# Score blocks for VectorE as four-column products of masked q, w2 on another queue, and a new plan of numbers

## The chip, the cores and the metric
The kernel runs on one core of a Trainium2 chip. The core has TensorE (PE; its weight loads are listed as PEld), VectorE (DVE), ScalarE (ACT), GpSimd (POOL) and SyncE (SP), which only issues DMAs here; ScalarE can issue DMAs on a queue of its own. All five run their own instruction streams and wait for each other by semaphores. The metric is the device time of one execution in microseconds (us); lower is better. The median before is 662.22 us.

## The reference, cut to what matters
```python
x = A_x                                  # 1 x 2048 x 512, bf16
xn = layernorm(x)
q = (xn @ wq), 32 heads of 16            # scale 16 ** -0.5 on the scores
k, v = xn @ wk, xn @ wv                  # one head of 16, shared by all 32
p = softmax(q @ k.T)                     # 32 heads x 2048 x 2048 scores
s = (p @ v, heads side by side) @ wo
g = silu(silu(xn @ w1) @ w2)             # 512 -> 1792 -> 512
out = x + s * g
```
The softmax has 134 million exponentials. They are the bulk of the work outside TensorE.

## The kernel before, in words
The queries are cut into 4 column blocks of 512 (c), and the heads into groups of four, which gives 8 groups a block and 32 groups (gi) in all. In a group, head i of four lies on partitions 32i to 32i+31 of `qT_sb`, 16 of them its own; a pair of groups shares the 32 partitions, and `kT_sb` exists twice (`kTa`, `kTb`), with k on the lower or the upper 16 of each 32 and zeros elsewhere, so that the even group of a pair is met by kTa and the odd one by kTb. `kTb` is made by small DMAs from `kTa` (`move_K`, L501).

For each group, keys come in 16 tiles of 128 (kt). A *block* is the scores of one head, one key tile and 512 queries, keys on the partitions: one matmul with 32 contracted rows at row position 32i (`score`, `burst`, L613). Two blocks fill one of the two halves psA0, psA1 of PSUM and are exponentiated by one ScalarE instruction of 1024 columns into one of NPA slots of `pa_sb` (`exp_A`, L643; "an exp" below). Other key tiles go to VectorE: four blocks of one tile, each in one of the banks D, D1 (psD) or F (psF), are turned by one add with an int16 output into bits of a bf16 power of two (`exp_D`, L681); GpSimd makes two shifted copies of the four (`shift`, L706, INT64_ADD), and the three weighted copies together stand for the exponential. The probabilities never leave the core: each block is multiplied with v (and a column of weights for the sum) into psO, 32 columns for each of the four heads side by side (`emit_PV`, L765). Four such matmuls, one per head, make a *quad*; they use the four column positions of TensorE at once, while score matmuls use the four row positions. The PE stream is therefore a sequence of *score runs* (row form: one psA half and one or two blocks for VectorE that ride along) and *stretches* between them (column form: value quads and pieces of the dense work).

The dense work (q of the next block, h = xn @ w1, z = u @ w2, the output product w) is cut into four-column products as well (`columns`, L392) and fills the stretches, through bank F. Its silu takes a tanh on ScalarE (L1081) and products on VectorE (L1113, L1125, then the addition of x, L1092, and a store from `ob_sb`).

Nothing of this order is written out by hand. The class `Sched` records every operation with what it reads and writes, gives it a planned time from fixed costs, and derives the semaphores. The main loop (L1353 on) decides at each step, by those planned times, how many quads and dense pieces go into the next stretch, which blocks ride in the next run, and what VectorE does next. A string `PLAN` names a row of `RULES` for every 5 us of planned time; a row holds the thresholds for these decisions (waiting times, how many stretches to keep ahead, how much dense work may lag, and so on). Changing a number therefore changes the order of thousands of instructions.

DMAs are recorded the same way and go to SP's queue in the recorded order: the kTb moves, w1, the late loads (`late_loads`: wo, w2; both on SP), reloads of x, and the stores. `fill_D` (L1308) picks the VectorE blocks that ride in a run; `extra_fill` (L1288) can put one between runs, in row form; `col`-form filling of VectorE blocks doesn't exist.

## Time and profile before
| | |
|---|---|
| Median of 3 runs | 662.22 us (661.94 to 662.23) |
| The profiled execution | 662.46 us, of which its span (first to last instruction) 660.6 us |
| ScalarE busy | 652.5 us, 99%; 662 exps at 1217 ns mean, 72 tanhs at 797 ns mean |
| TensorE busy | 648.8 us, 98% |
| VectorE busy | 597.3 us, 90% |
| GpSimd busy | 382.9 us, 58% |
| Granted TensorE clock | 1.00 |
| First exp starts, last exp ends | 10.21 us, 653.23 us |

The page gives for each engine the time in which at least one of its instructions ran. ScalarE and TensorE overlap the end of one instruction with the start of the next, so their mean durations are longer than the distance from one to the next, and a share near 100% still can hide short waits. The chain of waits goes back from the last instruction to what released each step; a line of it gives the start, the length and what ran, so its steps show distances and not durations. "Idle before" is the time an engine stood still ahead of an instruction, with what ended it.

### The profile page before, as it was taken

Reading aid. Unit: us, or ns where it says so; the run is one execution under the profiler, and the core shown is the slowest. Engines: PE = TensorE matmul, PEld = TensorE weight load, DVE = VectorE, ACT = ScalarE, POOL = GpSimd, SP = SyncE. Lnnn points to the kernel's source line nnn. Section 1 sums busy time; section 2 is a strip of 40 time slices with the busy share of each in tenths; the row PEclk is TensorE's granted clock in tenths of the full one; section 3 lists DMA queues with packets and bytes.
Section 4 is the critical chain, followed back from the end, with each engine's and each line's share of the span. In section 5 each row is a group of like instructions: output and inputs, shape, how many; then the busy total and the mean of one; then the engine's idle time right before and its main releaser. Section 6 shows DMA issues by size and latency. Waiting matters only on the chain.

```text
span 660.6 us, 18424 instructions
## 1 busy us (share of the span) xinstructions
PE 648.8 (98%) x8061; PEld 182.9 (28%) x8061; DVE 597.3 (90%) x1021; ACT 652.5 (99%) x754; POOL 382.9 (58%) x387
## 2 busy tenths in 40 slices
PE   8999999999999999999999999999999999999996
PEld 4422222222222222222222222222222222222222
DVE  7998899998899989999998989999989888898996
ACT  8999999999999999999999999999999999999997
POOL 3265666655566567566656655575656555665554
PEclk9999999999999999999999999999999999999999
DMA  5440000000000000000000000010000000000110
GB/s 167 153 147 1 2 1 2 2 1 2 2 1 2 17 18 18 17 2 2 1 2 1 2 1 2 2 33 18 18 1 3 1 2 2 1 2 2 33 34 33
DMA packets 12320, 12.48 MB, mean 19 GB/s; under 512 B 2512, under 2 KB 11728, under 8 KB 12240
## 3 DMA queue, kind: packets, MB, share of 16 engines
q1 hardware_dynamic: 11680, 10.78, 5.3%
q8 instruction: 63, 1.03, 0.7%
q10 hardware_dynamic: 560, 0.52, 0.2%
q14 instruction: 17, 0.14, 0.1%
HBM read 8.95 MB, written 2.10 MB: 17 GB/s over the span
## 4 chain that ended last, share of the span: by engine, by line
ACT 91%; PE 4%; DVE 2%; issue 1%; DMA 1%; SPq 1%; POOL 0%; POOLq 0%
ACT pa_sb L643 85%; ACT t_sb L1081 5%; PE psA L613 1%; DMA x_sb<-in_A_x_dram 1%; PE psO L765 1%; DVE ph_sb L681 1%; DVE stats_sb L408 0%; POOL ph_sb L706 0%; PE psD L452 0%; PE psF L392 0%; DMA kTb_sb<-kTa_sb 0%; SPq L501 0%; PE psD L483 0%; DVE kTa_sb L495 0%; POOLq L293 0%
## 5 line engine op out<-in xcount | busy, mean ns | idle before, releaser
L643 ACT ACTIVATE pa_sb<-psA 128x1024 bf16<-128x1024 f32 x662 | 630.5, 1217 | 0.9 <-PE psA L613 0.6
L706 POOL INT64_ADD ph_sb<-ph_sb x290 | 300.3, 1048 | 192.7 <-DVE ph_sb L681 192.6
L681 DVE TENSOR_SCALAR ph_sb<-psD 128x512 int16<-128x512 f32 (+1 forms) x520 | 349.1, 689 | 33.7 <-PE psD L613 29.8
L765 PE MATMUL psO<-ph_sb,vaug_sb 128*32 128x512 bf16 x1740 | 215.9, 383 | 0.1
L765 PE MATMUL psO<-pa_sb,vaug_sb 128*32 128x512 bf16 (+1 forms) x1332 | 200.2, 383 | 0.4 <-ACT pa_sb L643 0.4
L613 PE MATMUL psA<-qT_sb,kTa_sb 32*128 32x512 bf16 x688 | 133.4, 385 | 1.9 <-DVE kTa_sb L495 0.5
L613 PE MATMUL psD<-qT_sb,kTb_sb 32*128 32x512 bf16 x353 | 129.5, 384 | 0.0
L613 PE MATMUL psA<-qT_sb,kTb_sb 32*128 32x512 bf16 x628 | 121.7, 385 | 2.2 <-ACT pa_sb L643 1.7
L613 PE MATMUL psD<-qT_sb,kTa_sb 32*128 32x512 bf16 x309 | 111.6, 384 | 0.2
L706 POOL INT64_ADD x_sb<-x_sb x72 | 74.5, 1046 | 52.2 <-DVE x_sb L681 52.1
L681 DVE TENSOR_SCALAR x_sb<-psD 128x512 int16<-128x512 f32 (+1 forms) x132 | 90.1, 690 | 10.6 <-PE psD L613 8.9
L765 PE MATMUL psO<-x_sb,vaug_sb 128*32 128x512 bf16 x432 | 73.7, 383 | 0.0
L613 PEld LDWEIGHTS psA<-qT_sb,kTa_sb 32*128 32x128 bf16 x688 | 32.3, 91 | 141.8 <-ACT pa_sb L643 125.5
L392 PE MATMUL psF<-xnT_sb,w_sb 128*32 128x512 bf16 x896 | 71.1, 385 | 0.0
L392 PE MATMUL psF<-w_sb,u_sb 128*32 128x512 bf16 x896 | 69.2, 384 | 0.0
L613 PEld LDWEIGHTS psA<-qT_sb,kTb_sb 32*128 32x128 bf16 x628 | 29.5, 91 | 134.4 <-ACT pa_sb L643 124.4
L765 PEld LDWEIGHTS psO<-ph_sb,vaug_sb 128*32 128x32 bf16 x1740 | 52.5, 95 | 49.7 <-issue 34.1
L765 PEld LDWEIGHTS psO<-pa_sb,vaug_sb 128*32 128x32 bf16 x1332 | 48.1, 94 | 41.9 <-issue 32.1
L1081 ACT ACTIVATE t_sb<-psF 128x512 bf16<-128x512 f32 x72 | 57.4, 797 | 0.0
L1113 DVE SCALAR_TENSOR_TENSOR u_sb<-t_sb,psF 128x512 bf16<-128x512 bf16 x56 | 38.0, 679 | 4.7 <-ACT t_sb L1081 4.2
L681 DVE TENSOR_SCALAR ph_sb<-psF 128x512 int16<-128x512 f32 x52 | 35.4, 681 | 0.0
L613 PEld LDWEIGHTS psD<-qT_sb,kTb_sb 32*128 32x128 bf16 x353 | 30.9, 91 | 3.5 <-DVE ph_sb L681 2.5
(128 smaller groups left out, 341.6 us busy)
## 6 DMA issues: line engine op xcount, KB each, us to landing
w_sb<-in_B_w_dram SPq DMA_DIRECT2D x2, 1792.0 KB, 8.8
x_sb<-in_A_x_dram SPq DMA_DIRECT2D x18, 128.0 KB, 2.3
out_dram<-ob_sb SPq DMA_DIRECT2D x14, 128.0 KB, 1.7
x_sb<-in_A_x_dram SPq DMA_DIRECT2D x3, 512.0 KB, 7.1
wop_sb<-in_A_wo_dram SPq DMA_DIRECT2D x1, 512.0 KB, 4.0
wq_sb<-in_A_wq_dram SPq DMA_DIRECT2D x1, 384.0 KB, 6.6
x_sb<-in_A_x_dram ACTq DMA_DIRECT2D x2, 128.0 KB, 2.9
kTb_sb<-kTa_sb SPq DMA_DIRECT2D x16, 16.0 KB, 2.3
```

The lines of the kernel that those rows point to most:

```text
L392: r = e.matmul(bank[32 * i:32 * i + 32, :], lhsT=lhsT[:, 32 * i:32 * i + 32], rhs=rhs, start=start, stop=stop, tile_position=(0, 32 * i), ...
L613: return e.matmul(ap, lhsT=kT_sb[g % 2][32 * i:32 * i + 32, kt * P:(kt + 1) * P], rhs=qT_sb[32 * i:32 * i + 32, c % 2, g // 2, :], start=T ...
L643: d = op("a", lambda e: e.activation(pa_sb[:, sl, :], psA[k][:, :], ACT.Exp, scale=ESCALE), reads=["A%d" % k], writes=[("pa", sl)], cost=2 ...
L681: d = op("v", lambda e: e.tensor_scalar(ph_ap(0, sl, 512 * pos, 512 * pos + m), src, float(PH_ONE + PH_BIAS), 0.0, op0=ALU.add, op1=ALU.ma ...
L706: d = op("gp", lambda e, j=j: e.int64_add(ph_ap(j, sl, 0, 4 * NQ).bitcast(I64), ph_ap(0, sl, 0, 4 * NQ).bitcast(I64), PH_SHIFT[j] * 0x0001 ...
L765: r = e.matmul(psO[32 * i:32 * i + 32, cs], lhsT=vaug_sb[:, p["v"], p["kt"], :], rhs=p["ap"], start=s0, stop=s1, tile_position=(0, 32 * i) ...
L1081: op("a", lambda e: e.activation(t_sb[:, n % 2, :], bank_ap(b), ACT.Tanh, scale=0.5 if jb[0] == "h" else 0.25), reads=[b], writes=[("t", n ...
L1113: op("v", lambda e: e.scalar_tensor_tensor(out=dst, in0=t_sb[:, n % 2, :], scalar=1.0, in1=src, op0=ALU.add, op1=ALU.mult), reads=tk["read ...
```

## The change
Seven things are changed together:
- A tensor `qm_sb` [128, 4, 512] is added, zeroed once on GpSimd in the start. For each pair of groups four DMAs on SP (`mask_q`) copy head i's 32 rows of q into `qm_sb[32i:32i+32, i, :]`. The other rows stay zero, so a product over all 128 rows of kT with `qm_sb[:, i, :]` is head i's score block. It can be made in column form: four matmuls of 32 columns (`col_fill`, through `columns`).
- The main loop may put such a *column fill* into a stretch (`col_want` looks whether a bank is free and whether VectorE would have a block earlier by more than a threshold, CGAIN or CLEFT).
- The load of w2 is issued on ScalarE's queue instead of SP's.
- NPA goes from 11 to 10 slots.
- The gated result is written to `ob_sb` directly, and x is added to it there; `fin_sb` is gone.
- `held` counts by a dictionary (no instruction of the chip changes by that).
- PLAN and RULES are new, with two more numbers a row.

```diff
-    NPA = 11
+    NPA = 10
...
-        fin_sb = sb("fin_sb", [P, 2, D])
+        qm_sb = sb("qm_sb", [P, 4, NQ])
...
+        op("gp", lambda e: e.memset(qm_sb[:], 0.0), writes=[("qm", i) for i in range(4)], cost=1.8)
...
-            op("sp", lambda e: e.dma_start(w2_sb[:], B_w2.rearrange("(ft p) n -> p ft n", p=P)), writes=["w2"], lane="lw2", cost=9.0)
+            op("a", lambda e: e.dma_start(w2_sb[:], B_w2.rearrange("(ft p) n -> p ft n", p=P)), writes=["w2"], lane="lw2", cost=9.0)
...
-                op("v", lambda e: e.scalar_tensor_tensor(out=fin_sb[:, tt % 2, :], in0=src, scalar=0.25,
+                op("v", lambda e: e.scalar_tensor_tensor(out=ob_sb[:, tt % NOB, :], in0=src, scalar=0.25,
...
+        def mask_q(gi):
+            c, h = gi // NG, (gi % NG) // 2
+            for i in range(4):
+                op("sp", lambda e, i=i: e.dma_start(qm_sb[32 * i:32 * i + 32, i, :], qT_sb[32 * i:32 * i + 32, c % 2, h, :]),
+                   reads=[("qT", c % 2, h), "qTb"], writes=[("qm", i)], lane=f"qm{i}")
+            qm["of"] = gi // 2
...
+        def col_fill(w):
+            _, bank, o, i = w
...
+            def f(e):
+                return columns(e, bank_ap(bank), kT_sb[gi % 2][:, kt * P:(kt + 1) * P], qm_sb[:, i, :], True, True)
+            ks = [("kT", 1, kt // 2, n) for n in range(4)] if gi % 2 else [("kT", 0, kt // 2 if kt else "first")]
+            op("pe", f, reads=[("qm", i)] + ks, writes=[bank], cost=("col", [0, 1, 2, 3], NQ))
+            dst["fifo"].append(dict(tile=o["tile"], i=i, bank=bank, idx=idx, pos=pos, rows=o["rows"]))
+            hold[bank] = "blk"
+            return 1
...
+                w = col_want(t, CGAIN) if CGAIN < 9 and slots > did else None
+                k = int((w[0] - max(t, K.pe_next("col")) - 0.05) / 0.2163 + 0.8) if w else 9
+                if k <= 0:
+                    did += col_fill(w)
...
+                if CLEFT < 9 and slots > did:
+                    w = col_want(max(t, K.pe_next("col")), CLEFT)
+                    if w and w[0] <= max(t, K.pe_next("col")) + 0.1:
+                        did += col_fill(w)
```

More of the change, by code (lines that the diff above doesn't have):

```diff
@@ L254, in bass_recurrent_scan__grouped_kv_mqa__dense_activation_silu__prompt_kernel @@
     NPAIR, LEAD_PAIR = 1, 1
+    COLS, CGAIN, CLEFT = 1, 9, 9
     TWIN = 0
@@ L262, in bass_recurrent_scan__grouped_kv_mqa__dense_activation_silu__prompt_kernel @@
     PLAN = (
-        "AAAAJAVDBHQUALNMAMMPRULHALUHROAAMAKVIAVMMASMAAAAAFVIAAKAANJM"
-        "AGGHQLHSNAMAAGMPOCVAVAMAAVIAAHLAMRHIAFHKTOLENGTNLUAAAAPAPHRA"
-        "ESJA"
+        "AAAAHbEbOAZQHCFBAAYARBZMAVTAAAbMBZIYAUBWOQADVAJGPFTAUAHFXAGW"
+        "AABNWZAAFAYQaZQJXQbALZScFAACNZFANQZMGZZYAGAAAZVZQAAAAFZAAZKA"
+        "QA"
     )
     RULES = dict(
-        A=(0.2, 3.0, 0.65, 10, 1.2, 2.0, 0, 12, 0.2, 3, 3, 0.0, 9, 0.43, 0, 0.33, 0, 0),
-        B=(0.1, 3.0, 0.65, 10, 1.2, 2.0, 0, 12, 0.2, 3, 3, 0.0, 9, 0.43, 0, 0.33, 0, 0),
@@ L270, in bass_recurrent_scan__grouped_kv_mqa__dense_activation_silu__prompt_kernel @@
-        C=(0.3, 3.0, 0.65, 10, 1.2, 2.0, 0, 12, 0.2, 3, 3, 0.0, 9, 0.43, 0, 0.33, 0, 0),
-        D=(0.2, 3.0, 0.5, 10, 1.2, 2.0, 0, 12, 0.2, 3, 3, 0.0, 9, 0.43, 0, 0.33, 0, 0),
-        E=(0.2, 3.0, 0.65, 9, 1.2, 2.0, 0, 12, 0.2, 3, 3, 0.0, 9, 0.43, 0, 0.33, 0, 0),
-        F=(0.2, 3.0, 0.65, 11, 1.2, 2.0, 0, 12, 0.2, 3, 3, 0.0, 9, 0.43, 0, 0.33, 0, 0),
-        G=(0.2, 3.0, 0.65, 10, 1.2, 2.0, 4, 12, 0.2, 3, 3, 0.0, 9, 0.43, 0, 0.33, 0, 0),
-        H=(0.2, 3.0, 0.65, 10, 1.2, 2.0, 8, 12, 0.2, 3, 3, 0.0, 9, 0.43, 0, 0.33, 0, 0),
@@ L276, in bass_recurrent_scan__grouped_kv_mqa__dense_activation_silu__prompt_kernel @@
-        I=(0.2, 3.0, 0.65, 10, 1.2, 2.0, 0, 12, 0.2, 3, 3, 0.04, 9, 0.43, 0, 0.33, 0, 0),
-        J=(0.2, 3.0, 0.65, 10, 1.2, 2.0, 0, 12, 0.2, 3, 3, 0.0, 0.05, 0.43, 0, 0.33, 0, 0),
-        K=(0.2, 3.0, 0.65, 10, 1.2, 2.0, 0, 12, 0.2, 3, 3, 0.0, 0.15, 0.43, 0, 0.33, 0, 0),
-        L=(0.2, 3.0, 0.65, 10, 1.2, 2.0, 0, 12, 0.2, 3, 3, 0.0, 0.25, 0.43, 0, 0.33, 0, 0),
-        M=(0.2, 3.0, 0.65, 10, 1.2, 2.0, 0, 12, 0.2, 3, 3, 0.0, 0.35, 0.43, 0, 0.33, 0, 0),
-        N=(0.2, 3.0, 0.65, 10, 1.2, 2.0, 0, 12, 0.2, 3, 3, 0.0, 9, 0.43, 0.2, 0.33, 0, 0),
@@ L282, in bass_recurrent_scan__grouped_kv_mqa__dense_activation_silu__prompt_kernel @@
-        O=(0.2, 3.25, 0.65, 10, 0.6, 2.0, 0, 12, 0.2, 3, 3, 0.0, 0.05, 0.43, 0, 0.33, 0, 0),
-        P=(0.1, 2.5, 0.65, 10, 1.2, 2.0, 4, 12, 0.2, 3, 3, 0.0, 9, 0.43, 0, 0.33, 2, 0),
-        Q=(0.2, 2.5, 0.65, 10, 1.2, 2.0, 0, 12, 0.2, 3, 3, 0.0, 0.15, 0.43, 0, 0.33, 0, 0),
-        R=(0.2, 3.0, 0.65, 10, 1.2, 2.0, -12, 12, 0.2, 3, 3, 0.04, 9, 0.43, 0, 0.33, 0, 0),
-        S=(0.2, 3.0, 0.65, 10, 1.2, 3.0, 0, 6, 0.2, 2, 3, 0.0, 9, 0.43, 0, 0.33, 0, 0),
-        T=(0.2, 3.0, 0.65, 10, 1.2, 2.0, 0, 12, 0.2, 3, 2, 0.0, 9, 0.43, 0, 0.6, 2, 0),
@@ L288, in bass_recurrent_scan__grouped_kv_mqa__dense_activation_silu__prompt_kernel @@
-        U=(0.2, 3.0, 0.65, 10, 1.2, 2.0, 0, 12, 0.2, 3, 3, 0.0, 9, 0.55, 0, 0.33, 1, 0),
-        V=(0.2, 3.0, 0.65, 10, 1.2, 2.0, 0, 12, 0.2, 2, 4, 0.04, 9, 0.43, 0, 0.33, 0, 1),
+        A=(0.2, 3.0, 0.65, 10, 1.2, 2.0, 0, 12, 0.2, 3, 3, 0.0, 9, 0.43, 0, 0.33, 0, 0, 9, 9),
+        B=(0.2, 3.0, 0.65, 10, 1.2, 2.0, 0, 12, 0.2, 3, 3, 0.0, 9, 0.43, 0, 0.33, 0, 0, 0.4, 9),
+        C=(0.2, 3.0, 0.65, 10, 1.2, 2.0, 0, 12, 0.2, 3, 3, 0.0, 9, 0.43, 0, 0.33, 0, 0, 0.6, 9),
+        D=(0.2, 3.0, 0.65, 10, 1.2, 2.0, 0, 12, 0.2, 3, 3, 0.0, 9, 0.43, 0, 0.33, 0, 0, 0.8, 9),
@@ new lines, in bass_recurrent_scan__grouped_kv_mqa__dense_activation_silu__prompt_kernel @@
+        E=(0.2, 3.0, 0.65, 10, 1.2, 2.0, -12, 12, 0.2, 3, 3, 0.0, 9, 0.43, 0, 0.33, 0, 0, 9, 9),
+        F=(0.2, 3.0, 0.65, 10, 1.2, 2.0, 0, 12, 0.2, 3, 3, 0.0, 9, 0.43, 0.2, 0.33, 0, 0, 9, 9),
+        G=(0.2, 3.0, 0.65, 10, 1.2, 2.0, 0, 12, 0.2, 3, 3, 0.0, 9, 0.43, 0, 0.33, 1, 0, 9, 9),
+        H=(0.2, 3.0, 0.65, 10, 1.2, 2.0, 0, 12, 0.2, 3, 3, 0.0, 0.05, 0.43, 0, 0.33, 0, 0, 9, 9),
+        I=(0.2, 3.0, 0.65, 10, 1.2, 2.0, 0, 12, 0.2, 3, 3, 0.0, 9, 0.43, 0, 0.33, 2, 0, 9, 9),
+        J=(0.2, 3.0, 0.65, 7, 1.2, 2.0, 0, 12, 0.2, 3, 3, 0.0, 9, 0.43, 0, 0.33, 0, 0, 9, 9),
@@ new lines, in bass_recurrent_scan__grouped_kv_mqa__dense_activation_silu__prompt_kernel @@
+        K=(0.2, 3.0, 0.65, 10, 1.2, 2.0, 0, 24, 0.2, 3, 3, 0.0, 9, 0.43, 0, 0.33, 0, 0, 9, 9),
+        L=(0.2, 3.0, 0.65, 10, 1.2, 2.0, -8, 12, 0.2, 3, 3, 0.0, 9, 0.43, 0, 0.33, 0, 0, 9, 9),
+        M=(0.2, 3.0, 0.65, 10, 1.2, 2.0, 0, 12, 0.2, 3, 3, 0.0, 0.25, 0.43, 0, 0.33, 0, 0, 9, 9),
+        N=(0.25, 3.0, 0.6, 10, 1.2, 2.0, 0, 12, 0.2, 3, 4, 0.0, 9, 0.43, 0, 0.33, 0, 0, 0.6, 9),
+        O=(0.2, 3.0, 0.65, 10, 1.2, 2.0, 0, 12, 0.2, 3, 3, 0.0, 9, 0.43, 0, 0.15, 0, 0, 0.8, 0.05),
+        P=(0.25, 3.0, 0.65, 10, 1.2, 2.0, 0, 12, 0.2, 3, 3, 0.0, 0.35, 0.43, 0, 0.33, 0, 1, 9, 9),
@@ new lines, in bass_recurrent_scan__grouped_kv_mqa__dense_activation_silu__prompt_kernel @@
+        Q=(0.2, 2.75, 0.65, 10, 1.2, 2.0, 0, 12, 0.2, 3, 3, 0.0, 9, 0.43, 0.2, 0.33, 0, 0, 0.6, 9),
+        R=(0.2, 3.0, 0.65, 10, 1.2, 2.0, 0, 12, 0.2, 3, 3, 0.04, 9, 0.43, 0, 0.33, 2, 0, 9, 0.05),
+        S=(0.2, 3.0, 0.65, 10, 0.6, 2.0, 0, 12, 0.3, 3, 4, 0.0, 9, 0.43, 0, 0.33, 0, 0, 0.8, 9),
+        T=(0.2, 3.0, 0.65, 10, 1.2, 2.0, 0, 12, 0.2, 2, 3, 0.0, 9, 0.43, 0, 0.15, 0, 0, 9, 0.05),
+        U=(0.2, 3.0, 0.65, 10, 1.2, 2.0, 0, 12, 0.2, 3, 3, 0.04, 9, 0.43, 0, 0.33, 0, 0, 9, 0.4),
+        V=(0.2, 3.0, 0.65, 10, 1.2, 2.0, 0, 12, 0.2, 3, 4, 0.0, 9, 0.43, 0, 0.6, 0, 0, 0.4, 0.6),
@@ new lines, in bass_recurrent_scan__grouped_kv_mqa__dense_activation_silu__prompt_kernel @@
+        W=(0.2, 3.25, 0.65, 10, 1.2, 2.0, 0, 12, 0.2, 4, 3, 0.0, 9, 0.43, 0, 0.33, 0, 0, 0.6, 0.4),
+        X=(0.25, 3.0, 0.65, 10, 1.2, 3.0, 0, 12, 0.2, 3, 3, 0.0, 9, 0.43, 0, 0.6, 0, 0, 0.6, 0.4),
+        Y=(0.2, 2.75, 0.65, 10, 1.2, 1.5, 0, 12, 0.2, 3, 3, 0.0, 9, 0.43, 0, 0.33, 0, 0, 0.4, 9),
+        Z=(0.2, 3.0, 0.65, 10, 1.2, 3.0, 4, 12, 0.2, 3, 3, 0.0, 9, 0.43, 0, 0.15, 0, 0, 9, 0.05),
+        a=(0.3, 3.0, 0.65, 10, 1.2, 2.0, -4, 24, 0.2, 3, 3, 0.04, 9, 0.43, 0, 0.33, 0, 0, 9, 9),
+        b=(0.2, 3.25, 0.65, 10, 1.2, 2.0, 0, 12, 0.2, 4, 3, 0.04, 9, 0.43, 0, 0.33, 0, 1, 9, 9),
@@ L290, in bass_recurrent_scan__grouped_kv_mqa__dense_activation_silu__prompt_kernel @@
+        c=(0.2, 3.0, 0.7, 10, 1.6, 2.0, 0, 12, 0.2, 3, 3, 0.0, 9, 0.43, 0, 0.33, 0, 0, 0.6, 9),
     )
@@ L593, in bass_recurrent_scan__grouped_kv_mqa__dense_activation_silu__prompt_kernel @@
             halves[gi] = [(h, (2 * p, 2 * p + 1), rows) for h in range(2) for p in range(NPAIR) for rows in ([0, 1], [2, 3])]
-        pend = [[] for _ in range(NGRP)]
+        pend, waiting = [[] for _ in range(NGRP)], {}
         npv = [[0] * 4 for _ in range(NGRP)]
@@ L628, in held @@
         def held(key):
-            return any(p["key"] == key for q in pend for p in q)
+            return waiting.get(key, 0) > 0
         def owe(gi, i, kt, v, ap, key, at, half=None):
             pend[gi].append(dict(i=i, kt=kt, v=v, ap=ap, key=key, at=at, half=half))
+            waiting[key] = waiting.get(key, 0) + 1
         def fill_A(tile, rows, k):
@@ L754, in emit_PV @@
                     pend[gi] = [x for x in pend[gi] if x is not p]
+                    waiting[p["key"]] -= 1
                     owed[gi] -= 1
@@ L1054, in emit_job @@
                 else:
-                    task(k, evac, 0.69, jb=jb, bank=b, reads=[b], writes=[])
+                    task(k, evac, 0.69, jb=jb, bank=b, reads=[b], writes=[("ob", jb[1] % NOB)] if k == "w" else [])
                 if k in ("z", "w"):
@@ L1099, in add @@
             tt = tk["jb"][1]
-            final_add("v", tt, fin_sb[:, tt % 2, :], ("fin", tt % 2))
+            final_add("v", tt, ob_sb[:, tt % NOB, :], ("ob", tt % NOB))
             tok.add(("add", tt))
@@ L1124, in evac @@
                 tt = jb[1]
-                op("v", lambda e: e.scalar_tensor_tensor(out=fin_sb[:, tt % 2, :], in0=src, scalar=0.25,
+                op("v", lambda e: e.scalar_tensor_tensor(out=ob_sb[:, tt % NOB, :], in0=src, scalar=0.25,
                                                          in1=tmp_sb[:, (tt // 4) % 2, tt % 4, :],
                                                          op0=ALU.mult, op1=ALU.mult),
-                   reads=[b, ("tmp", tt % 8)], writes=[("fin", tt % 2)], cost=tk["cost"])
+                   reads=[b, ("tmp", tt % 8)], writes=[("ob", tt % NOB)], cost=tk["cost"])
                 tok.add(("wev", tt))
-                task("add", add, 0.42, jb=jb, reads=[("fin", tt % 2), ("x", 12 + tt % 4)], writes=[])
+                task("add", add, 0.42, jb=jb, reads=[("ob", tt % NOB), ("x", 12 + tt % 4)], writes=[])
             elif k == "wp":
@@ L1138, in bass_recurrent_scan__grouped_kv_mqa__dense_activation_silu__prompt_kernel @@
         dst = dict(open=[], idx=-1, fifo=[])
+        qm = dict(of=-1)
         ast = dict(tile=None, rows=None)
@@ L1306, in extra_fill, with col_want @@
             fill_D(best[0], [0, 1, 2, 3], [best[1]])
+        def mask_q(gi):
[4 more added lines that the diff above has]
+            qm["of"] = gi // 2
+        def col_want(t, least):
+            if front or group_A() >= NGRP or sum(held(("pa", k)) for k in range(NPA)) >= XHOLD:
+                return None
+            pick = next(((o, i) for o in dst["open"] for i in o["todo"]
+                         if o["tile"][0] // 2 == qm["of"] and K.ready("pe", [("qm", i)]) <= t), None)
+            if pick is None:
+                return None
+            vfree = K.free["v"] + 0.62 * len(dst["fifo"])
+            ride = max(needed(), t + 0.2) + 0.43
+            best = None
+            for b in BANKS:
+                if hold[b] is None and (b != "F" or not jobs or not behind(F_BEHIND) or not next_job(t)):
+                    r = max(t, K.ready("pe", [], [b]))
+                    gain = max(vfree, ride) - max(vfree, r + 0.43)
+                    if gain > least and (best is None or r < best[0]):
+                        best = (r, b) + pick
+            return best
+        def col_fill(w):
+            _, bank, o, i = w
+            (gi, kt), idx = o["tile"], o["idx"]
+            pos = len(o["rows"]) - len(o["todo"])
+            o["todo"].remove(i)
+            if not o["todo"]:
+                dst["open"].remove(o)
+            def f(e):
[5 more added lines that the diff above has]
+            return 1
         def fill_D(t, free, only=None):
@@ L1332, in fill_D @@
                         dst["open"].append(dict(tile=new, todo=list(rows), rows=rows, idx=dst["idx"]))
+                        if COLS and not front and new[0] // 2 > qm["of"] and all(x["tile"][0] // 2 == new[0] // 2 for x in dst["open"]):
+                            mask_q(new[0])
                         pick = [(dst["open"][-1], i) for i in free if i in rows] or [(dst["open"][-1], rows[0])]
@@ L1354, in bass_recurrent_scan__grouped_kv_mqa__dense_activation_silu__prompt_kernel @@
             (SLIP, ROUND, KEEP, HOLD, AGES["gn1"], AGE, F_BEHIND, ENDQ, PVWAIT, LEAD, AHEAD, MARGIN, XGAIN, AIM, TWIN,
-             TGATE, FRESH, JOINT) = \
+             TGATE, FRESH, JOINT, CGAIN, CLEFT) = \
                 RULES[PLAN[min(int(K.act_end / STRETCH), len(PLAN) - 1)]]
@@ L1404, in bass_recurrent_scan__grouped_kv_mqa__dense_activation_silu__prompt_kernel @@
                     did += 2
+                w = col_want(t, CGAIN) if CGAIN < 9 and slots > did else None
+                k = int((w[0] - max(t, K.pe_next("col")) - 0.05) / 0.2163 + 0.8) if w else 9
+                if k <= 0:
+                    did += col_fill(w)
                 if slots > did:
-                    did += emit_PV(max(t, K.pe_last + K.pe_len) + 0.08, slots - did)
-                if can and not dense_first and slots > did:
-                    did += emit_job(t, slots - did)
+                    did += emit_PV(max(t, K.pe_last + K.pe_len) + 0.08, min(k, slots - did) if k > 0 else slots - did)
+                if can and not dense_first and slots > did and k > 0:
+                    did += emit_job(t, min(k, slots - did))
+                if w and k > 0 and slots > did and w[0] <= K.pe_next("col") + 0.12:
+                    did += col_fill(w)
+                    if slots > did:
+                        did += emit_PV(max(t, K.pe_last + K.pe_len) + 0.08, slots - did)
+                if CLEFT < 9 and slots > did:
+                    w = col_want(max(t, K.pe_next("col")), CLEFT)
+                    if w and w[0] <= max(t, K.pe_next("col")) + 0.1:
+                        did += col_fill(w)
             if TWIN and more and not blocked and did and not front and tanh_ready(K.act_end - TWIN):
```

## The prediction
> **What bounds the kernel now.** I read the page's busy line first, then the groups, the busy time by stretches, the chain of waits and the DMA view by window.

> ```profile
> span 660.6 us, 18424 instructions
> PE 648.8 (98%) x8061; PEld 182.9 (28%) x8061; DVE 597.3 (90%) x1021; ACT 652.5 (99%) x754; POOL 382.9 (58%) x387
> ...
> L643 ACT ACTIVATE pa_sb<-psA 128x1024 bf16<-128x1024 f32 x662 | 630.5, 1217 | 0.9 <-PE psA L613 0.6
> ...
> L1081 ACT ACTIVATE t_sb<-psF 128x512 bf16<-128x512 f32 x72 | 57.4, 797 | 0.0
> ```

> ScalarE is 99% busy, nearly all of it 662 exponentials (exps, L643) and 72 tanhs. By stretches (PE, PEld, DVE, ACT, POOL, clock, DMA, GB/s):

> ```profile
> 40.00:140.00 100.00, 99.23 (x1225) 27.55 (x1226) 92.44 (x156) 100.00 (x117) 59.36 (x58) 1.00 0.03 9
> ...
> 540.00:640.00 100.00, 99.79 (x1280) 26.49 (x1276) 91.04 (x149) 100.00 (x113) 60.03 (x58) 1.00 0.04 12
> sum 600.00, PE 596.28 PEld 162.46 DVE 548.66 ACT 600.00 POOL 360.24; mean PE 99.38 PEld 27.08 DVE 91.44 ACT 100.00 POOL 60.04
> ```

> For 600 us ScalarE is never idle. But a mean of 1217 ns hides gaps below 0.3 us: an exp starts before the one ahead has ended. The pitch tells them, so I take it from the chain, and count the start against it in ScalarE's timeline (the line by itself):

> ```profile
> 26.98 0.62 PE psF L452 x8
> 27.60 0.33 PE psO L765 x4
> 27.93 0.32 PE psA L613 x2
> ...
> 32.84 1.80 DMA kTb_sb<-kTa_sb
> ...
> 34.69 0.39 PE psF L613
> 35.08 0.33 PE psO L765 x4
> 35.40 0.32 PE psA L613 x2
> ...
> 35.78 17.51 ACT pa_sb L643 x19
> 53.29 0.49 ACT t_sb L1081
> ...
> 610.15 25.67 ACT pa_sb L643 x28
> ```

> ```profile
> 10.21 35.75 ACT L643 ACTIVATE pa_sb<-psA 128x1024 bf16<-128x1024 f32 x38 [0.59 <-PE psA L613]
> ```

> Pitch of an exp: 25.67 / 28 = 0.917 us; a tanh adds 0.49. The 38 exps from 10.21 would take 1.02 (the first one's own row) + 37 x 0.917 = 34.95; they took 35.75, so 0.8 us of stalls. From 45.96 to the last exp's end at 653.23 lie 624 exps and 72 tanhs: 572.2 + 35.3 = 607.5 against 607.3: no stall at all. The span is therefore head 10.2 + exps and tanhs 642.2 + stalls 0.8 + tail 7.3. Two stalls show their cause in the chain. The exp fed by the run at 27.93 came 0.23 late: transposes (0.62) and a value quad (0.33) stood ahead of its score run. The one fed at 35.40 came 0.14 late: TensorE waited at 34.64 for a kTb move to land.

> **The change, part by part.**
> *ScalarE's and VectorE's work.* The order of the built program has the same 662 exps, 72 tanhs, 724 blocks for VectorE (704 single evacuations and 10 pairs before, 708 and 8 after) and 362 INT64_ADDs. VectorE takes no block more than before; so 642.2 us stay: 0.
> *48 column fills.* 48 of the 724 single score matmuls outside psA become four 32-column products (192 matmuls, L392's helper), in the stretch of the value quads instead of riding in the score run. Price in TensorE time from the chain: a run is 0.32, a stretch of quads 0.33 for one and 0.22 for each further one (x4 0.33, x8 0.55). From exp 47 on, the order has 1387 quads in 615 gaps before (2.26 each) and 1433 after (2.33): 0.32 + 0.33 + 0.22 x 1.26 = 0.93 grows to 0.94 a gap. A gap has 0.917 + 72/615 x 0.49 = 0.974. Over stretches of 50 gaps the fullest had 98% before (gaps 546 to 595, no stall) and 98% after (gaps 296 to 345): ScalarE hides it, 0.
> *The two stalls.* In the new order the value quad ahead of the late run is gone (0.33 less, more than the 0.23), and the first block that needs the last kTb move stands four exps later (3.7 us): -0.23 - 0.14 = -0.37.
> *Tail.* Before, a value quad (0.22) stood between the last score run and the products for VectorE's first half of the last normalisation; after it stands earlier. That half starts 0.22 sooner, but the second half needs the last exp (653.23) and its product (653.29 + 0.40), so it starts at 653.74 instead of 653.87: -0.13. The last INT64_ADD pair stands two exps earlier; POOL is not the end.
> *w2 on ScalarE's queue*, after 23 exps, at about 30.7 us. No row shows ScalarE issuing between two exps. Lower end 0: an issue takes 0.51 (SP's row for w2) and the pitch is 0.917. Upper end: the issue waits for the datapath, 0.51 + the lost overlap 0.30 = 0.8. I take 0, by the exps' own rows: the next one is handed over 0.30 before the last has ended, so the queue runs ahead.
> *64 mask copies on SP* (32 KB each, 0.59 to issue by the kTb moves; four take 2.4 us, and the last lands 1.8 after its issue). In SP's queue only stores and x reloads stand between the batches, and what waits behind a mask is those. A mask can go once the pair before has read its row for the last time; by the order its first use comes 8 exps (7.3 us) or more after that, so the 2.4 + 1.8 are hidden, except in the first four. Those meet loads:

> ```profile
> kTb_sb<-kTa_sb SPq DMA_DIRECT2D x4, 16.0 KB, 5.0
> ...
> kTb_sb<-kTa_sb SPq DMA_DIRECT2D x4, 16.0 KB, 1.8
> ```

> The moves issued behind the w1 load (17.84 us) took 5.0 to land, those with nothing before them (31.02) 1.8. The first masks now stand behind wop, and w2 runs beside wop. Before, w2 (issued at 34.1, landed after 9.6) moved its 1.8 MB in the 6.2 us after wop's landing at 37.5: 300 GB/s. Started at about 32, some 1.1 MB of it are left when wop's 0.5 MB start at 34.5. The four x tiles at the start, two on each queue, landed alike (2.7 and 2.9 us), so I let the queues share: at half the rate wop lands at about 38.9 and the second mask at about 39.3. Its use stands ahead of the 33rd exp's run, which may start at 39.2 (11.23 + 30 x 0.917 + 0.45 of stalls). Estimate: the run is late by 0.45, of which some 0.1 is slack: +0.35. Lower end 0 (the loads don't slow each other: mask at 37.9). Upper end: masks behind all of w2, as the moves behind w1: about 41, +1.8. I take 0.35, by the x tiles. The last four kTb moves run beside w2 too; they are first needed at about 38 now, 3.4 after today's landing, and cost only in that upper case, in the same hole. [...]
> *Memset of qm on POOL*: 1.80 by kTb's, from 5.24 (wkp's copy ends) to 7.04, in the head:

> ```profile
> 3.09 1.80 POOL L377 MEMSET kTb_sb<- 128x2048 bf16 x1
> 4.84 0.40 POOL L379 COPY wkp_sb<-wkn_sb 128x256 bf16<-128x256 bf16 x1
> ...
> 6.13 1.38 DVE L441 TENSOR_SCALAR xn_sb<-x_sb,mv_sb,rstd_sb 128x512 bf16<-128x512 bf16 x4
> ```

> POOL's next work is at 11.41, so on POOL 0. But the four normalisations at 6.13, on the path to the first exp, now lie inside it. Lower end 0: kTb's memset ran beside three BATCH_NORM_STATS2 at the usual 0.69. Upper end: all VectorE work waits for 7.04, 0.91, and with the reciprocal at 5.91 about 1.1. I take 0, the memset's own row being the nearest; the other case is a rival.
> *The rest* goes together: ob instead of fin (same 12 + 12 instructions; the store four tiles back lands in 1.7 us, tiles are microseconds apart), NPA 10 (a slot comes round after 9 us), the counter in held (host only): 0.
> Sum: -0.37 - 0.13 + 0.35 = -0.15 on the profiled execution's 662.46 (span 660.6 and 1.9 around it): 662.3. It stands 0.24 above the median of the three runs, 662.22; so I predict 662.1 for a median.

> **The rivals.**
> *POOL's memset holds VectorE in the head.* For: VectorE's SBUF products (L853) range from 407 to 793 ns, and POOL is busy beside them. Against: the kTb memset's row. It gives 662.1 + 0.9 = 663.0, still within the bound below. [...]
> *The issue of w2 holds ScalarE*: 662.1 + 0.8 = 662.9. Against: the overlap of the exps.
> *Column fills make TensorE late (slower).* The view of waits (us in total, times, longest) has weight loads for psD standing for VectorE to free the bank, 0.25 each:

> ```profile
> PEld psD L613 <- DVE ph_sb L681: 6.7, 27, 0.4
> ```
>  Today they stand behind psA's run and delay no exp; a column fill stands ahead of it. It decides once some six of the 48 are held by that 0.25 with no slack left (1.5 us); with a quarter of them, 12 x 0.25 = 3.0: 665.1. For: gaps are 97% full where the fills are dense. Against: fuller gaps ran without a stall.
> *Faster.* The change doesn't do what it says, in the sense that VectorE's share does not grow. To win 1.3 us it would have to save all stalls (0.8), the tail's 0.13 and 0.4 more, for which I see no place: 660.8.

> **How the numbers follow.** 0.2% is 1.3 us, about what a measurement of this kernel can tell from no change. Likeliest case 0.52 (662.1); memset 0.22 (663.0); w2's issue 0.08 (662.9); slower rival 0.15 (665.1); faster 0.03 (660.8). The first three lie within 0.2%: 0.82. Range: downwards the sum without the 0.35 and 0.3 more of the early stalls (661.4), upwards the memset's and the masks' upper parts together (663.5); outside lie the slower and the faster case, 0.18.

> **What would show it.** ScalarE's chain unbroken at 0.917 from some 45 us on; ten or so first exps alike; no late exp near 29 and 37, one of 0.3 near 40 with TensorE waiting for a qm copy; first exp at 10.2 (11.1 if the memset holds). Wrong would be: exps late by 0.1 to 0.4 all along, behind products that read qm, with VectorE as releaser; or a hole of 0.8 at about 31.

## The result, and the profile after

The changed kernel takes 666.98 us (median of five runs, 664.41 to 668.03), against 661.94 (661.81 to 662.23) before: ratio 1.0069, 95% interval 1.0047 to 1.0092. It is slower, and its runs spread over 3.6 us where those of before spread over 0.4. The prediction said 662.1, no change. Three single runs far off the others (801.64 us with w2 later, 686.62 with both mends, 982.71 with w2 alone on ScalarE's queue), at a mean clock of 0.66 to 0.85, stand in no median or range below.

The page of the kernel after, busy times, granted clock and the two groups that make up ScalarE's work:

```profile
span 665.2 us, 18816 instructions
...
PE 652.6 (98%) x8199; PEld 184.7 (28%) x8201; DVE 597.5 (90%) x1023; ACT 652.6 (98%) x754; POOL 384.2 (58%) x388
...
PEclk9979999999999999999999999999999999999999
...
L653 ACT ACTIVATE pa_sb<-psA 128x1024 bf16<-128x1024 f32 x662 | 630.9, 1220 | 5.0 <-PE psD L622 2.8
...
L1092 ACT ACTIVATE t_sb<-psF 128x512 bf16<-128x512 f32 x72 | 57.8, 803 | 0.0
```

The numbers of instructions are as forecast, 662 and 72. The idle time ahead of the exps went from 0.9 to 5.0 us, and one slice of the clock row reads 7. ScalarE's timeline (start, us, engine, line, operation, xcount, idle before) says where:

```profile
10.80 20.28 ACT L653 ACTIVATE pa_sb<-psA 128x1024 bf16<-128x1024 f32 x22 [0.59 <-PE psA L622]
30.92 8.41 ACT L653 ACTIVATE pa_sb<-psA 128x1024 bf16<-128x1024 f32 x9
40.39 1.02 ACT L653 ACTIVATE pa_sb<-psA 128x1024 bf16<-128x1024 f32 x1 [1.07 <-PE psD L622]
43.00 1.02 ACT L653 ACTIVATE pa_sb<-psA 128x1024 bf16<-128x1024 f32 x1 [1.58 <-PE psA L622]
44.94 1.02 ACT L653 ACTIVATE pa_sb<-psA 128x1024 bf16<-128x1024 f32 x1 [0.92 <-PE psD L622]
46.46 1.02 ACT L653 ACTIVATE pa_sb<-psA 128x1024 bf16<-128x1024 f32 x1 [0.50 <-PE psD L622]
47.82 7.44 ACT L653 ACTIVATE pa_sb<-psA 128x1024 bf16<-128x1024 f32 x8 [0.34 <-PE psD L622]
```

Five exps in a row are late, by 1.17, 1.69, 1.02, 0.60 and 0.44 us against the pitch of 0.917: 4.93 us, "the hole" below. The other 728 exps and tanhs keep the pitch to 0.01 us, from the first at 10.80 to the last, which ends at 657.95. The books: first exp later by 0.59 (10.80 for 10.21); early stalls gone, -0.80; hole +4.93; tail 7.24 for 7.34, -0.10. That makes 4.62, and the spans differ by 665.2 - 660.6 = 4.6.

What TensorE waited for at 36 to 50 us (total, times, longest), and then the stretches with busy time of each engine, granted clock, DMA share and GB/s:

```profile
PE psD L401 <- DMA qm_sb<-qT_sb: 1.1, 1, 1.1
PE psF L622 <- DMA kTb_sb<-kTa_sb: 0.8, 1, 0.8
```

```profile
36.00:38.00 2.00, 2.00 (x24) 0.50 (x21) 1.83 (x3) 2.00 (x3) 0.70 (x2) 1.00 1.10 368
38.00:40.00 2.00, 1.10 (x11) 0.33 (x9) 0.95 (x2) 1.33 (x2) 1.98 (x2) 1.00 1.09 344
40.00:42.00 2.00, 0.88 (x15) 0.27 (x11) 1.74 (x3) 1.02 (x1) 0.00 (x0) 0.67 0.30 72
42.00:44.00 2.00, 2.00 (x18) 0.40 (x14) 0.85 (x2) 1.00 (x1) 0.74 (x1) 0.50 0.13 33
44.00:46.00 2.00, 2.00 (x18) 0.35 (x14) 1.03 (x2) 1.04 (x2) 1.31 (x2) 0.50 0.13 33
46.00:48.00 2.00, 2.00 (x22) 0.37 (x19) 1.43 (x4) 1.21 (x2) 0.00 (x0) 0.63 0.06 16
48.00:50.00 2.00, 2.00 (x33) 0.45 (x25) 1.82 (x4) 2.00 (x3) 0.49 (x1) 1.00 0.00 0
```

Two waits for DMAs, 0.80 us for a kTb move (until 39.32) and 1.12 for a mask (until 41.80). From 42 to 46 nothing is waited for, TensorE is busy all the time, and still it is too slow: its granted clock is 0.50, and a matmul of 0.39 us takes 0.60. The hole has a first part that is waiting and a second that is a clock. The DMA view of 30 to 46 us (KB each, median us from issue to landing) shows what the waits are made of:

```profile
w_sb<-in_B_w_dram ACTq DMA_DIRECT2D x1, 1792.0 KB, 9.5
wop_sb<-in_A_wo_dram SPq DMA_DIRECT2D x1, 512.0 KB, 7.9
...
qm_sb<-qT_sb SPq DMA_DIRECT2D x8, 32.0 KB, 3.8
kTb_sb<-kTa_sb SPq DMA_DIRECT2D x4, 16.0 KB, 5.9
```

Before, the same four kTb moves took 1.8 and wop 4.0:

```profile
wop_sb<-in_A_wo_dram SPq DMA_DIRECT2D x1, 512.0 KB, 4.0
```

ScalarE reached its issue of w2 at 30.89 us, just ahead of the moves (SP, 31.01 to 32.83); w2 landed at 40.36, the moves at 36.23 to 39.27 instead of 32.98 to 34.64, wop at 41.40 instead of 37.49, and the four first masks, behind wop in SP's queue, at 41.58 to 42.10. What the two queues moved from 33.5 to 40.4 us (q10 is ScalarE's, q1 is SP's; packets, MB, busy share of the DMA engines) says why:

```profile
q10 hardware_dynamic: 1553, 1.57, 71.7%
q1 hardware_dynamic: 791, 0.68, 32.6%
```

Until 36.3 SP's queue got next to nothing, 0.02 MB beside 0.85, though the four moves and wop were waiting in it. The head shows the other 0.59:

```profile
5.19 1.80 POOL L389 MEMSET qm_sb<- 128x2048 bf16 x1
...
6.04 2.06 DVE L450 TENSOR_SCALAR xn_sb<-x_sb,mv_sb,rstd_sb 128x512 bf16<-128x512 bf16 x4
```

The four normalisations took 1.38 before the change and 2.06 now, beside the memset.

### The profile page after: what moved, and what is told of

It is laid out like the page before. It is cut to its first block, busy times and chain, and to the rows that moved or that the text cites. A ratio compares the mean times of both kernels' runs of the same rounds, so it can differ in the third digit from the quotient of the medians.

```text
span 665.2 us, 18816 instructions
## 1 busy us (share of the span) xinstructions
PE 652.6 (98%) x8199; PEld 184.7 (28%) x8201; DVE 597.5 (90%) x1023; ACT 652.6 (98%) x754; POOL 384.2 (58%) x388
## 4 chain that ended last, share of the span: by engine, by line
ACT 77%; PE 17%; DVE 3%; DMA 1%; SPq 1%; issue 0%
ACT pa_sb L653 72%; PE psO L776 6%; PE psA L622 6%; ACT t_sb L1092 5%; PE psF L401 4%; DMA qm_sb<-qT_sb 1%; DVE stats_sb L417 1%; PE psD L461 0%; DMA x_sb<-in_A_x_dram 0%; DVE xn_sb L450 0%; SPq L510 0%; PE psD L492 0%; DVE kTa_sb L504 0%; PE psA L669 0%; DVE ph_sb L691 0%
## 5 line engine op out<-in xcount | busy, mean ns | idle before, releaser
L622 PE MATMUL psA<-qT_sb,kTb_sb 32*128 32x512 bf16 x632 | 123.1, 387 | 1.1 <-ACT pa_sb L653 0.6
L622 PE MATMUL psD<-qT_sb,kTb_sb 32*128 32x512 bf16 x325 | 114.7, 386 | 0.1
L691 DVE TENSOR_SCALAR x_sb<-psD 128x512 int16<-128x512 f32 x132 | 89.2, 684 | 12.6 <-PE psD L622 10.0
L622 PE MATMUL psD<-qT_sb,kTa_sb 32*128 32x512 bf16 x287 | 99.9, 384 | 0.0
L776 PE MATMUL psO<-x_sb,vaug_sb 128*32 128x512 bf16 x432 | 77.6, 383 | 0.0
L622 PEld LDWEIGHTS psD<-qT_sb,kTb_sb 32*128 32x128 bf16 x325 | 27.5, 91 | 2.0 <-DVE ph_sb L691 1.1
```

What stands on the lines that cost most here:

```text
L622: return e.matmul(ap, lhsT=kT_sb[g % 2][32 * i:32 * i + 32, kt * P:(kt + 1) * P], rhs=qT_sb[32 * i:32 * i + 32, c % 2, g // 2, :], start=T ...
L691: d = op("v", lambda e: e.tensor_scalar(ph_ap(0, sl, 512 * pos, 512 * pos + m), src, float(PH_ONE + PH_BIAS), 0.0, op0=ALU.add, op1=ALU.ma ...
L776: r = e.matmul(psO[32 * i:32 * i + 32, cs], lhsT=vaug_sb[:, p["v"], p["kt"], :], rhs=p["ap"], start=s0, stop=s1, tile_position=(0, 32 * i) ...
```

## The experiments

Theory A: w2, put where it runs beside SP's transfers, makes the kTb moves and the first masks late; TensorE waits, and its clock falls. Theory M: POOL's memset holds the first normalisations. The main rival is C, the one that the prediction feared: the column fills, or the new numbers, make TensorE late by themselves.

**w2 back on SP's queue** (that part undone).

```diff
-            op("a", lambda e: e.dma_start(w2_sb[:], B_w2.rearrange("(ft p) n -> p ft n", p=P)), writes=["w2"], lane="lw2", cost=9.0)
+            op("sp", lambda e: e.dma_start(w2_sb[:], B_w2.rearrange("(ft p) n -> p ft n", p=P)), writes=["w2"], lane="lw2", cost=9.0)
```

> The changed kernel with one part undone: w2 is issued on SP's queue again, behind wop and ahead of the first masks. Theory A (the loss at 38 to 48 us comes from what w2 does to the transfers beside and behind it): the four last kTb moves land by 34.7 and wop by 37.5 as before the change, so the wait of 0.80 at 38.5 goes; but the four first masks now queue behind w2, which landed at 43.71 in the kernel before, so they land at 44 to 45 and TensorE waits about 5 us for the first product at 39. One hole of 4.5 to 7 us instead of 4.93, with the clock falling in it: 666 to 669. Rival B (it is enough that w2 leaves ScalarE's queue): no hole, 662. Rival C (the products themselves or the new numbers make TensorE late, w2 has no part): five late exps of 4.9 in all at the same places, 666.5 to 667.

Measured 670.29 us, ratio 1.0122 (1.0108 to 1.0135): slower than the changed kernel. The kTb moves landed after 1.8 us and wop after 4.1, as before the change; the masks, issued from 35.77 on, landed at 45.53 to 45.98, right behind w2 (45.38). TensorE's timeline has one wait:

```profile
45.72 0.62 PE L401 MATMUL psD<-qm_sb,kTb_sb 128*32 128x512 bf16 x4 [5.21 <-DMA qm_sb<-qT_sb]
```

Exps late by 7.88 in all: 5.65 behind this wait, then 1.02, 0.60 and 0.60 at a clock of 0.50. The first exp came at 11.93 in this run. Both hole and head are more than theory A had given, 4.5 to 7 us and no change, so the time is above its 666 to 669. Rival B falls: on SP w2 stands ahead of the masks, on ScalarE's queue it runs beside what is ahead of them. Rival C's five late exps at the old places aren't there either. Both cost the hole.

**w2 later**, the queue kept, nothing else moved (`state["n"]` counts the exps; the load leaves `late_loads`).

```diff
+        def load_w2():
+            op("a", lambda e: e.dma_start(w2_sb[:], B_w2.rearrange("(ft p) n -> p ft n", p=P)), writes=["w2"], lane="lw2", cost=9.0)
...
+            if state["n"] == 40:
+                load_w2()
```

> The changed kernel with w2 still on ScalarE's queue but issued 17 exps later, after the 40th exp (about 47 us), when the kTb moves, wop and the first masks have landed; all other instructions on all engines keep their order. Theory A (w2 beside the loads makes the kTb moves and the first masks late, TensorE waits twice and then runs at half clock): last kTb move lands by 34.7, wop by 37.5, first masks by 39.3, no wait over 0.3 us on TensorE, clock 1.00 throughout, late exps at most 0.3 in all; time 662.0 + 0.6 (head) - 0.8 - 0.1 = 661.7, 0 to 0.3 more, and the spread of the runs falls from 3.6 us to some 0.5. Rival C (products or new numbers make TensorE late): the hole stays, 666 to 667. Rival D (the issue of w2 on ScalarE costs an exp, hidden in the hole so far): one exp late by 0.5 to 0.8 at about 47, 662.3 to 662.7.

Measured 663.07 us (ratio 1.0019, 1.001 to 1.0028). In the profiled run the hole is gone: no exp late by more than 0.01 from the first to the last, clock 1.00, moves 1.9, wop 4.3. ScalarE's timeline up to the issue of w2:

```profile
11.71 35.87 ACT L655 ACTIVATE pa_sb<-psA 128x1024 bf16<-128x1024 f32 x39 [0.59 <-PE psA L624]
47.42 0.39 ACTq L398 DMA_DIRECT2D w_sb<-in_B_w_dram  x1
```

The 39 exps are 1.02 and 38 pitches of 0.917, with none late. So rival C falls, and with it D: w2's issue between two exps costs nothing. But 661.7 was missed by 1.4, and most of the spread (662.09 to 664.79) stayed. Runs of 664.10 to 664.79 have a mean clock of 0.996 or 0.997, the others 0.998 to 1.000; no profile shows what their clock did. The profiled run (662.97) has its first exp at 11.71, and the head shows why:

```profile
6.00 3.02 DVE L452 TENSOR_SCALAR xn_sb<-x_sb,mv_sb,rstd_sb 128x512 bf16<-128x512 bf16 x4
...
6.51 0.47 POOL L387 COPY wkp_sb<-wkn_sb 128x256 bf16<-128x256 bf16 x1 [1.61 <-DMA wkn_sb<-in_A_wk_dram]
...
6.94 1.94 POOL L389 MEMSET qm_sb<- 128x2048 bf16 x1
```

The memset stands behind a copy that waits for wkn. In this run wkn landed at 6.46, in the changed kernel's profile at 4.67; the memset then begins in the middle of the four normalisations, which take 3.02 us instead of 1.38 beside its 1.94. Its price is not 0.59 but whatever the landing of wkn makes of it: 0.59 there, 1.50 here, 1.72 in the run with w2 on SP (wkn at 6.43).

**The memset later**, behind the eighth normalisation (in `ln_nm`).

```diff
-        op("gp", lambda e: e.memset(qm_sb[:], 0.0), writes=[("qm", i) for i in range(4)], cost=1.8)
...
+            if t == 7:
+                op("gp", lambda e: e.memset(qm_sb[:], 0.0), reads=[("xn", 7)], writes=[("qm", i) for i in range(4)], cost=1.8)
```

> The changed kernel with POOL's memset of qm put behind the eighth normalisation instead of ahead of the first four; nothing else moves. Theory M (the memset slows the four normalisations from 1.38 to 2.06 us and so the first exp by 0.59): the four take 1.38 again, first exp at 10.2 instead of 10.8; the hole at 38 to 48 us stays, since the loads are issued when they were: 0.4 to 0.8 under the changed kernel, in so far as its runs repeat to that (666.4 of 667.0). The memset may then slow the normalisation or another VectorE instruction that it meets later, without an exp late. Rival N (something else in the new order makes the first exp late): first exp at 10.8 still, same time.

Measured 666.66 us (663.80 to 667.45), 0.3 under the changed kernel, which the spread of either doesn't resolve. The normalisations take 1.38 again and the first exp starts at 10.15; the hole stays, 5.55 us of late exps from 40.02 on. Theory M holds for the head. One of the four runs took 663.80, with a mean clock of 0.999 instead of 0.994 or 0.995: there the second part of the hole seems to be missing.

**The memset alone, in the kernel before.**

```diff
+        op("gp", lambda e: e.memset(wop_sb[:], 0.0), writes=["wop"], cost=1.8)
```

> The kernel before with one thing added: POOL sets as many bytes to zero as qm has, at the same place in its queue (behind the copy into wkp). They go into wop's tile, which is loaded at 33 us. Theory M (the memset and the four first normalisations shut each other out, for as long as the memset still runs when it meets them; when it starts hangs on the landing of wkn, 4.5 to 6.5 us): the four normalisations take 2.0 to 3.1 instead of 1.38, first exp 0.6 to 1.6 later: 662.6 to 663.7, with a spread of over 0.8 us. Rival N (the memset does nothing, the later first exp belongs to the new order): 662.1, spread of 0.4.

Measured 662.58 us against 662.15, ratio 1.0013 (1.0004 to 1.0022); ten runs, seven of them 662.52 to 662.61, the others 663.66, 663.68 and 664.97. In the profiled run (662.52) wkn landed at 4.50, the four normalisations take 1.95, and the first exp starts at 10.79 (10.21 before). Two of the forecasts are missed by little, the 2.0 of the normalisations and the 662.6. So the memset costs 0.4 in the median and now and then 1.5 or more, without any other part of the change.

**w2 on ScalarE's queue alone, in the kernel before.**

```diff
-            op("sp", lambda e: e.dma_start(w2_sb[:], B_w2.rearrange("(ft p) n -> p ft n", p=P)), writes=["w2"], lane="lw2", cost=9.0)
+            op("a", lambda e: e.dma_start(w2_sb[:], B_w2.rearrange("(ft p) n -> p ft n", p=P)), writes=["w2"], lane="lw2", cost=9.0)
```

> The kernel before, with one part of the change alone: w2 issued on ScalarE's queue behind the 23rd exp, instead of on SP's behind wop. No masks, no column fills, the old numbers per stretch. Theory A (w2 beside SP's transfers makes them late): the four last kTb moves, landed by 34.64 before, land between 36 and 39.5 as in the changed kernel; here TensorE wants them at 34.7 already, so it waits about 4.5 us, one exp is late by 4 to 4.6, the granted clock falls to about 0.5 for 6 us or more, and three or four further exps are late by 0.6 to 1.0: 667 to 669.5, slower than the changed kernel itself. Rival C (the products or the new numbers are the cause, w2 alone does nothing): 662.1, chain unbroken from 45 us on.

Measured 669.06 us (668.23 to 669.23), ratio 1.0102 (1.0086 to 1.0117). The profile is of a repetition:

> The same kernel as the one before with w2 alone moved to ScalarE's queue, once more for a profile, since the one taken was of a run of 982.71 us whose loads and exps stood elsewhere. Its three other runs are at 668.23 to 669.23. Theory A: kTb moves land between 36 and 39.5 beside w2, TensorE waits for them from 34.7, one exp late by 4 to 4.6 and three or four more by 0.6 to 1.0 at a clock near 0.5: late exps of 6.5 to 7.5 in all beside the 0.7 that stood there before, 668 to 669.5. Rival G (w2's issue or its landing holds ScalarE, DMA has no part): late exps with no releaser on TensorE, kTb landed by 34.7.

668.89 us (668.77 and 669.02), ratio 1.0099 (1.0069 to 1.0128). TensorE's timeline, and three of the stretches:

```profile
37.65 0.60 PE L613 MATMUL psD<-qT_sb,kTb_sb 32*128 32x512 bf16 x1 [3.76 <-DMA kTb_sb<-kTa_sb]
38.43 0.60 PE L613 MATMUL psF<-qT_sb,kTb_sb 32*128 32x512 bf16 x1 [0.18 <-DMA kTb_sb<-kTa_sb]
```

```profile
34.00:36.00 2.00, 0.00 (x0) 0.00 (x0) 0.04 (x1) 1.27 (x2) 1.86 (x2) 0.73 1.06 373
...
40.00:42.00 2.00, 2.00 (x22) 0.51 (x19) 1.38 (x2) 1.77 (x2) 0.00 (x0) 0.50 0.04 12
42.00:44.00 2.00, 2.00 (x19) 0.24 (x11) 0.77 (x2) 1.08 (x2) 1.92 (x2) 0.50 0.00 0
```

This one line of the change, by itself, costs 6.6 us (668.89 against 662.33 measured beside it), more than the whole change, because the old order wants the last kTb moves at about 34 and the new one at 38.5. The moves landed at 34.99 to 38.39; exps late by 5.00, then 0.17, 1.02, 0.60 and 0.20. SP's queue starves here too: 0.02 MB beside 1.15 on ScalarE's from 32 to 36 us. There is not one product with a mask in this kernel.

**Zeros for TensorE in both waits**: the kernel with the later memset, and 16 and 20 products with zeros into the two banks that the waiting matmuls overwrite. `keep_warm` does it once for each name and leaves the planned times as they were, so that the order stays.

```diff
+        def keep_warm(n, when, bank):
...
+            def f(e):
+                for _ in range(n):
+                    r = columns(e, bank_ap(bank), zero_sb[:, 0:P], zero_sb[:, :], True, True)
+                return r
+            op("pe", f, reads=["zero"], writes=[bank], cost=("col", [0, 1, 2, 3] * n, NQ))
...
+                if bank == "F" and o["tile"][0] % 2:
+                    keep_warm(4, "kTb", bank)
                 burst([((o["tile"], i), bank_ap(bank))], [bank])
...
+            keep_warm(5, "qm", bank)
```

> The changed kernel with the memset of qm behind the eighth normalisation (so that the head is still, as in the run with that alone: 666.66) and with TensorE given products with zeros where it waits: 16 32-column matmuls into the bank that the score block from kTb is about to overwrite, and 20 into the bank of the first product with qm. The loads and their landing are unchanged; only TensorE isn't idle. Theory A2 (of the 5 to 5.5 us in the hole a part is the two waits themselves, the rest is the clock that falls after them): clock 1.00 at 40 to 50 us, the first two late exps stay (1.0 to 1.2 each) and the ones behind them go: 2.2 to 2.8 us of late exps in all, 663.5 to 664.5. Rival E (the clock falls for another cause than TensorE's idle time, or its fall costs nothing of itself): the clock falls to 0.5 as before and five to six exps are late, 666 to 667.5.

Measured 664.58 us (663.75 to 665.86), ratio 1.0039 (1.0025 to 1.0053), in the median 2.1 under the same kernel without zeros, though the ranges of the two overlap. The loads are as late as ever (kTb moves to 38.33, wop 41.03), but:

```profile
38.00:40.00 2.00, 2.00 (x29) 0.68 (x32) 1.34 (x2) 0.76 (x1) 1.41 (x2) 1.00 1.03 306
40.00:42.00 2.00, 1.82 (x30) 0.65 (x27) 1.36 (x3) 1.02 (x1) 0.00 (x0) 1.00 0.09 26
42.00:44.00 2.00, 2.00 (x28) 0.54 (x26) 1.41 (x3) 1.62 (x2) 1.20 (x2) 1.00 0.18 46
```

The clock stays at 1.00, in the mean of all four runs too, and late are three exps by 1.36, 1.39 and 0.17: 2.92, where the kernel without zeros had 5.55. The zeros themselves hold TensorE for some 0.6 us past the landing of the last move (38.33; the block starts at 38.93), but the wait for the mask until 41.56 comes after that, so they don't lengthen the sum. Theory A2 holds, the sum a little above its 2.2 to 2.8: somewhat over half of the hole are the two waits, the rest is the clock that TensorE's idle time takes away. Rival E falls.

**Both mends**: w2 after the 40th exp, the memset behind the eighth normalisation.

> The changed kernel with both: w2 issued after the 40th exp on ScalarE's queue, and the memset of qm behind the eighth normalisation. Theories A and M together: first exp at 10.2, no late exp over 0.2, clock 1.00, tail 7.24: 10.2 + 642.2 + 0.1 + 7.2 = 659.7 of span, 661.1 to 661.5 in time, 0.6 to 1.0 under the kernel before, so under both kernels. Rival C: 666, with the hole. Rival D (the issue of w2 costs ScalarE 0.5 to 0.8): 661.8 to 662.1, no better than the kernel before.

Measured 661.57 us (661.42 to 662.45), ratio 0.9993 (0.9984 to 1.0002): 0.1 above the forecast's upper end, and not told apart from the kernel before. The spread is 1.0 us, where w2 late alone left 2.7. First exp at 10.31, no hole, and three early exps late by 0.43 in all.

**w2 on SP, behind the first masks**, memset late (`load_w2` with "sp", called once in `mask_q` behind its four DMAs).

```diff
+            if qm["of"] < 0:
+                load_w2()
             qm["of"] = gi // 2
```

> As the run with both mends, but w2 on SP's queue, right behind the first four masks, and not on ScalarE's after the 40th exp. Theory A (what counts is which transfers w2 goes ahead of or beside, not whose queue it is on): masks land by 39.5 as there, w2 by about 44, the second masks behind it by 45 to 46, first used at 57.7; no late exp but the three early ones (0.43): 661.4 to 661.9. Rival F (w2 in flight at all at 37 to 44 us takes something from the products with qm or their masks): late exps at 39 to 46, over 663.

Measured 661.48 us (661.29 to 662.15), ratio 0.9992 (0.9983 to 1.0001). ScalarE's timeline:

```profile
10.25 39.53 ACT L654 ACTIVATE pa_sb<-psA 128x1024 bf16<-128x1024 f32 x43 [0.59 <-PE psA L623]
```

43 exps in 39.53 us are 1.02 and 42 pitches of 0.917, not one late; nor is any later one. First masks landed at 37.41 to 38.11, w2 at 44.98, in flight all through the stretch of the old hole. Rival F falls: it isn't the queue, but what w2 runs beside or ahead of. This is the best version found, 5.5 us under the changed kernel; from the kernel before (662.15) it can't be told apart for certain (the interval reaches 1.0001).

**Column fills off**, all else as in the changed kernel.

```diff
-    COLS, CGAIN, CLEFT = 1, 9, 9
+    COLS, CGAIN, CLEFT = 0, 9, 9
...
-             TGATE, FRESH, JOINT, CGAIN, CLEFT) = \
+             TGATE, FRESH, JOINT, _, _) = \
```

> The changed kernel with the column fills and the masks switched off; the new numbers per stretch, NPA 10, w2's place and the memset stay. Its order has 679 exps where both kernels have 662, since without the products VectorE is left with 17 exps' worth fewer blocks under these numbers. Theory H (numbers and products belong together: the products give back what the new numbers alone would cost): 17 x 0.917 = 15.6 more of exps; the wait for the first mask goes, the one for kTb may stay: 676 to 683. Rival I (the products are worth nothing, the numbers alone carry the new order): 662 to 667 in spite of the exps, which would need the pitch to be shorter than 0.917.

Measured 682.01 us (681.82 and 682.20). The span is 15.2 longer than the changed kernel's: 17 exps are 15.6, the hole is 2.67 instead of 4.93 (-2.3), and head, two later stalls and tail add 0.66, 0.82 and 0.37. Theory H holds: under the new numbers the fills carry 17 exps, and these numbers are of no use without them. Of the hole this kernel keeps one wait alone, 0.83 us for kTb until 39.52, and one wait is enough for the clock:

```profile
38.00:40.00 2.00, 1.17 (x12) 0.31 (x4) 0.55 (x2) 1.99 (x3) 1.41 (x2) 1.00 1.07 345
40.00:42.00 2.00, 2.00 (x17) 0.52 (x16) 2.00 (x4) 1.02 (x1) 0.64 (x1) 0.89 0.26 83
42.00:44.00 2.00, 2.00 (x18) 0.39 (x19) 1.33 (x4) 1.09 (x2) 0.77 (x1) 0.50 0.00 0
44.00:46.00 2.00, 2.00 (x22) 0.33 (x14) 1.74 (x4) 1.65 (x2) 1.28 (x2) 0.75 0.00 0
```

## Why the prediction was wrong

*ScalarE's and VectorE's work, 0; 48 column fills, 0; the issue of w2, 0; the rest, 0.* Right. The pitch held everywhere outside the hole, and with w2 and the memset moved no exp at all was late behind a column fill. The slower rival (TensorE late behind VectorE's banks, 665.1) gave the right sign by a cause that no run shows.

*The two stalls, -0.37, and the tail, -0.13.* Right: both stalls are gone and the tail is 0.10 shorter. The 0.43 at 13 to 19 us come and go from run to run in these kernels (0.43 with w2 late on ScalarE's queue, 0 with it on SP), so the profile's -0.80 is not all the change's.

*Masks behind the loads, +0.35, at most +1.8.* This is the step that failed, in three places.
- "I let the queues share: at half the rate wop lands at about 38.9". It landed at 41.40. From 33.5 to 40.4 us, ScalarE's queue moved 1.57 MB and SP's 0.68: 30%, not half; and until 36.3 SP's had 0.02 of 0.87 MB. So w2 went nearly first, and wop and the masks landed only after it (40.36), much as in the case that the prediction kept for its upper end, masks behind all of w2. The x tiles that the price was taken from are equal pairs of 128 KB at the start; w2 is 1792 KB in one piece.
- "The last four kTb moves ... cost only in that upper case". They were late in the ordinary case, 16 KB each landing after 5.2 to 6.4 us instead of 1.8, and were the first of the two waits. Why SP's queue got 30% of the bytes, and 0.02 of 0.87 MB at first, no run shows: the cause of this division stays open.
- The bound of 1.8 held only waits. The two waits by themselves come to about 2.9 us of late exps (the run with zeros), and the clock adds 2 to 2.6. The sum had no term for the clock. The top of the range doesn't follow from the prediction's own parts either: the memset's 0.9 and the masks' 1.45 (1.8 less 0.35) on top of 662.1 make 664.45, not 663.5, and the measured time lies above both.

*Memset of qm on POOL, 0.* Wrong, and the rival was right in kind: 0.59 in the profile, 0.9 foreseen, up to 1.7 where wkn lands late. The row taken, kTb's memset beside three BATCH_NORM_STATS2 at the usual 0.69, shows another instruction that doesn't mind. Four normalisations of 0.35 us each on average (1.38 in all before) took 3.02 with w2 late, 1.64 more, beside the memset's 1.94. In the changed kernel one of the four, begun at 6.04 while the memset ran (5.19 to 6.99), lasted 1.10, and the other three 0.40 each. Why the memset holds these and not the BATCH_NORM_STATS2, no run shows.

With the measured terms the prediction's own sum comes out: 662.46 - 0.80 - 0.10 + 4.93 + 0.59 = 667.1, against 666.98. The range failed for the same reason as the sum; the prediction's one late exp "of 0.3 near 40 with TensorE waiting for a qm copy" names the right wait, but the exp behind that wait was late by 1.69, and four others were late with it.
